# Gathers ahead of scatters, and new places for the re-layout of a mixture-of-experts block's tokens

## The chip, the cores and the metric

One core of a Trainium2 chip runs the program. The metric is the device time of one execution in microseconds (us). Five engines run instruction streams of their own, each in order: TensorE (PE, matmuls; its weight loads are listed as PEld), VectorE (DVE), ScalarE (ACT), GpSimd (POOL) and SyncE (SP, which here only issues DMA transfers). They meet at semaphores.

## The reference, cut to what matters

```python
x = A_x                                # 2048 tokens x 512
xn = layernorm(x)
return x + linear_attention(xn, A_wqkv, A_wo) + moe(xn, B_w_gate, B_w1, B_w2)

def moe(xf, w_gate, w1, w2):           # 8 experts, 512 -> 1792 -> 512, top 2 of 8
    logits = xf @ w_gate
    topk_idx = argsort(-logits)[:, :2]
    gates = softmax(top-2 logits)
    for e in range(8):
        w = (gates * (topk_idx == e)).sum(-1)
        out += w * (silu(xf @ w1[e]) @ w2[e])
```

## The kernel before, in words

The first 200 us are layer norm, linear attention and routing. Then come the experts, taken in the order of their token counts: **rank** r = 0 to 7, with room for 576, 552, 544, 528, 520, 512, 512 and 512 tokens (`CAP`). A rank has four blocks of 128 tokens, and ranks 0 to 4 a small fifth (`single(r)` is true where there is none).

The hidden width of 1792 is worked off in seven **pairs** j = 0 to 6 of 2 x 128 columns. From the third pair of the program on, one pair is `pair_fast` (line 1103): seven products of the first matmul by a Strassen-like scheme (PSUM tiles px, pz, px, pz, px, py, px, lines 1115), and between them pieces of the second matmul of the pair before (`mm2`, tiles y, lines 1044 and 1047). After product k it calls `jobs(k)`: the list of **slot** k (0 to 6), into which `plan` (line 1352) puts, with `on(k, f, ...)`, everything else of that stretch: splitting weights into a high and a low part, fetching weights, and the next rank's tokens. So a list written out by hand sets the order of the work on every queue; nothing is reordered later. The product py (line 1115, started after slot 4) writes into a PSUM tile that pz held, so it waits until DVE's line 1137 has read pz; that DVE instruction stands between slots 2 and 3.

The tokens of rank r + 1 are brought in during rank r, block by block (i = 0 to 4):
- `gather1` (line 899, the DMA at 904): an indirect DMA on POOL's queue fetches 128 rows from DRAM into a tile xg (pairs 0 and 1).
- `x_out` (line 954, DMAs at 959): SP stores the block to DRAM in four pieces of 64 KB, in another order (xs_d).
- `x_gate` (line 927, DVE at 933 and 934): two tiny DVE instructions take the block's gate values out of xg. `x_out` calls it at its end.
- `x_in` (line 964, DMA at 969): SP loads the block back, 256 KB, as xq; it can leave SP only when the block's stores have landed.
- `x_turn` (line 971, DVE at 978): two DVE 32x32 transpositions give the transposed operand xr.
- `x_hi`, `x_lo`, `x_sum` (pairs 4 to 6) make the operands of the products from xr.

The results go the other way. `put` (line 1013) scales a block of y by its gates into a tile yo, and POOL adds it to the output with an indirect scatter (line 1021). Rank r - 1's first two blocks (all four, for a rank of four blocks) are put at the start of pair 1 of rank r, the others (transposed first, `y_out`, line 1073) at the start of pairs 2 and 3. POOL works its queue in order: a gather behind a scatter waits until the scatter's data are there.

The tiles xg, xq and yo share one set of 11 buffers (`ta`, line 88). Weights go through three 512 KB staging buffers (`wst`); `fetch_w` (line 795) issues the next load on SP as soon as slot 4 (`w1_p_lo`) or slot 6 (`w2_lo`) has emptied one. All these DMAs of SP share one queue, in the order of issue.

Of the kernel before, what the change touches and what calls it, by code (L numbers as in the profile page):

```python
# [47 lines left out]
NP = NF // 2  # L48
NPLAIN = 2
BLK = 32  # L50
PRODUCTS = (("A11", "B11"), ("S1", "T1"), ("S2", "T2"), ("S4", "B22"),
            ("S3", "T3"), ("A12", "B21"), ("A22", "T4"))

# [6 lines left out]
def linear_attn_plus_moe(  # L60
# [46 lines left out]
    def psm(tag, name, n=512):  # L107
        bufs = {"acc": 4, "mm": 2, "tr": 2}[tag]
        t = ps.tile([P, 512], F32, tag=tag, name=name, bufs=bufs)
        return t[:, :n]  # L110
# [771 lines left out]
    def single(r):  # L882
        return CAP[r] == 4 * P

    def half(r):
        return CAP[r] // 2
# [8 lines left out]
    xg = {}  # L895
# [17 lines left out]
    def width(r, i):  # L913
        return P if i < 4 else CAP[r] - 4 * P

    def turned(r, q):
        if (r, "B11") not in XR:
            n = half(r)
            np_ = -(-CAP[r] // BLK) * BLK
            for q_ in range(2):  # L920
                t = raw(um(f"xr{r}_{q_}"))[:, :2 * np_].rearrange("p (k c) -> p k c", k=2)
                XR[r, q_] = t
                for c in range(2):
                    XR[r, f"B{q_ + 1}{c + 1}"] = t[:, :, c * n:(c + 1) * n]
        return XR[r, q]

    def x_gate(r, i):
        if i == 4 and single(r):
            return
        g, w = xg[r, i], width(r, i)  # L930
        b = r * RB + i
        g8 = wp.tile([P, E], F32, tag="g8", name=f"g8_{b}", bufs=2)
        V.tensor_tensor(g8[:w], g[:w, D:], ohr[:w, r, :], op=ALU.mult)
        V.tensor_reduce(gate[:w, b:b + 1], g8[:w], axis=AX.X, op=ALU.add)  # L934

    def x_block(r, i, tag="tr"):
        if i == 4 and single(r):
            return
        g, w = xg[r, i], width(r, i)
        p = psm(tag, f"xep{r}_{i}")  # L940
        for kc in range(KC):
            T.transpose(p[:, kc * P:(kc + 1) * P], g[:, kc * P:(kc + 1) * P], ident)
        p = p.rearrange("p (k c) -> p k c", k=KC)
        for q in range(2):
            A.activation(turned(r, q)[:, :, i * P:i * P + w], p[:, 2 * q:2 * q + 2, :w], AF.Copy)
        x_gate(r, i)
        xg.pop((r, i))

    xq = {}

    def groups(r, i):
        return -(-width(r, i) // BLK)

    def x_out(r, i):
        if i == 4 and single(r):
            return
        b = r * RB + i
        for c in range(groups(r, i)):
            Q.dma_start(xs_d[b * P:(b + 1) * P, c * P:(c + 1) * P].rearrange("(a j) f -> j a f", j=BLK),
                        xg[r, i][c * BLK:(c + 1) * BLK, :D].rearrange("p (a f) -> p a f", f=P))  # L960
        x_gate(r, i)
        xg.pop((r, i))

    def x_in(r, i):
        if i == 4 and single(r):
# [5 lines left out]
    def x_turn(r, i):  # L971
        if i == 4 and single(r):
            return
        ng = groups(r, i)
        src = xq.pop((r, i))[:, :ng * P].rearrange("p (c i k) -> p c k i", i=BLK, k=KC)
        for q in range(2):
            dst = turned(r, q)[:, :, i * P:i * P + ng * BLK].rearrange("p k (c j) -> p c k j", j=BLK)
            V.transpose(dst, src[:, :, 2 * q:2 * q + 2, :])  # L978
# [94 lines left out]
    def y_out(r, k, tag="mm"):  # L1073
        if single(r):
            return
        i, o, w = by_column(r)[k]
        p = psm(tag, f"yp{r}_{k}")
        for d in range(KC):
            T.transpose(p[:w, d * P:(d + 1) * P], yt[r, d // 2][:, d % 2, o:o + w], ident)  # L1079
        put(r, i, p, w, A)  # L1080
# [22 lines left out]
    def pair_fast(r, j, fill, jobs, held):  # L1103
# [5 lines left out]
        def product(k, ps_, start):  # L1109
            wn, xn_ = PRODUCTS[k]  # L1110
            which, o = WPOS[wn]
            w, x = W1[r, j][which], XF[r, xn_]
            for kc in range(2):
                for i, (a, b) in enumerate(PASSES):
                    T.matmul(ps_, w[a][:, o + kc, :], x[b][:, kc, :],  # L1115
                             start=(start and kc == 0 and i == 0), stop=(kc == 1 and i == 2),
                             skip_group_check=True)
# [92 lines left out]
    def q_transp(t):  # L1210
        p = psm("tr", f"pqp{t}")
        for kc in range(KC):
            T.transpose(p[:, kc * P:(kc + 1) * P], pz[t][:, kc * P:(kc + 1) * P], ident)  # L1213
        pqT[t] = sm(f"pqT{t}").rearrange("p (h c) -> p h c", h=2)
        split(pqT[t][:, 0], pqT[t][:, 1], p)
# [74 lines left out]
    for t in range(OLAG + 1, NT - 2):  # L1290
# [14 lines left out]
        if t == 12:  # L1305
            x_block(0, 0)
        if t == 13:
            x_block(0, 1)
            gather1(0, 4)
# [17 lines left out]
        if t == 13:  # L1327
            x_block(0, 2)


    t = NT - 2
# [20 lines left out]
    def plan(g):  # L1352

        r, j = pairs[g]
        at = [[] for _ in range(7)]
        front = []

        def on(k, f, *args):
            at[k].append(lambda: f(*args))

        if g + 1 < len(pairs) and g + 1 >= NPLAIN:
            nx = pairs[g + 1]
            on(0, w1_s_hi, *nx, 0)
            on(1, w1_s_hi, *nx, 1)
            on(1, w1_s_lo, *nx, 0)
            on(2, w1_s_lo, *nx, 1)
            on(2, w1_p_hi, *nx, 0)
            on(3, w1_p_hi, *nx, 1)
            on(3, w1_p_lo, *nx, 0)
            on(4, w1_p_lo, *nx, 1)  # L1370
        if g > 0:
            on(3, w2_hi, r, j, 0)
            on(4, w2_hi, r, j, 1)
            on(5, w2_lo, r, j, 0)
            on(6, w2_lo, r, j, 1)
        if g + 2 < len(pairs) and g + 2 >= NPLAIN:
            nx = pairs[g + 2]
            on(5, w1_sums, *nx, 0)
            on(6, w1_sums, *nx, 1)
        if g == 0:  # L1380
            for k, name in enumerate(("T1", "T3", "T2", "T4")):
                on(k, x_sum, 0, name)
        if g in (0, 1):
            for k, name in enumerate((("T1", "T2"), ("T3", "T4"))[g]):
                on(4 + k if g == 0 else 2 * k, x_hi, 0, name)
                on(5 + k if g == 0 else 2 * k + 1, x_lo, 0, name)
        if r + 1 < E:
            for i in {0: (0, 1), 1: (2, 3, 4)}.get(j, ()):
                on(1 + i, gather1, r + 1, i)
            for i in {1: (0, 1), 2: (2, 3, 4)}.get(j, ()):  # L1390
                on(0, x_out, r + 1, i)
                on(3, x_in, r + 1, i)
            for k, i in {2: ((1, 0), (2, 1)), 3: ((1, 2), (2, 3)), 4: ((0, 4),)}.get(j, ()):
                on(k, x_turn, r + 1, i)
            steps = {4: ((1, x_hi, "B11"), (4, x_hi, "B22"), (5, x_lo, "B11"), (6, x_sum, "T1")),
                     5: ((0, x_lo, "B22"), (0, x_sum, "T3"), (1, x_hi, "B21"), (4, x_hi, "T1"),
                         (5, x_lo, "B21"), (5, x_sum, "T2"), (6, x_lo, "T1")),
                     6: ((0, x_sum, "T4"), (1, x_hi, "T2"), (3, x_hi, "T3"), (4, x_hi, "T4"),
                         (5, x_lo, "T2"), (6, x_lo, "T3"))}
            for k, f, name in steps.get(j, ()):  # L1400
                on(k, f, r + 1, name)
        if r > 0 and j == 0:
            on(0, x_lo, r, "T4")
        if r > 0 and not single(r - 1):
            for k in {2: (0, 1), 3: (2,)}.get(j, ()):
                front.insert(k % 2, lambda k=k: y_out(r - 1, k))
        if j == 3 and r in (E // 2, E - 1):
            on(0, G.drain)
        if r == E - 1:
            if j == 2:  # L1410
                on(0, m_in)
            if 2 <= j < 5:
                for k in (0, 1):
                    if NO + 2 * (j - 2) + k < NT:
                        on(1 + k, pz_in, NO + 2 * (j - 2) + k)
            if j >= 4:
                for k in (0, 1):
                    if NO + 2 * (j - 4) + k < NT:
                        front.append(lambda k=k: q_transp(NO + 2 * (j - 4) + k))
        return at, front  # L1420
# [3 lines left out]
    held = None  # L1424
    for g, (r, j) in enumerate(pairs):
        at, front = plan(g)
        first = len(rest)
        todo = rest + (pieces(*pairs[g - 1]) if g else [])
# [110 lines left out]
```

## Time and profile before

| | |
|---|---|
| Median of 3 runs (lowest, highest) | 853.36 us (852.06, 854.20) |
| Profiled execution: its time, its span | 853.94 us, 852.30 us |
| PE busy | 837.9 us (98%) |
| DVE, ACT, POOL busy | 80%, 63%, 21% |
| Mean granted TensorE clock | 0.996 |
| DMA | 124.18 MB, mean 146 GB/s |

The span runs from the first to the last instruction; the execution's own time is 1.6 us longer. A row of a timeline gives the start and the length of an instruction (of several in a row, where it says xN), its engine and line, what it writes and reads, and in brackets how long the engine had been idle before it and what ended that. SPq is SP's sequencer issuing a DMA. Matmuls overlap: the length of one is more than the distance to the next.

### The profile page before, as it was taken

The numbers are of one execution on the slowest core, as the hardware profiler recorded it, in microseconds if no ns is written. First come the engines' busy times: TensorE is split into PE (matmuls) and PEld (weight loads), VectorE is DVE, ScalarE is ACT, GpSimd is POOL, SyncE is SP. The second block draws the span as 40 slices with busy tenths as digits, with TensorE's granted clock in tenths as the row PEclk, the third lists the DMA queues.
The fourth block names the chain that finished last, engine by engine and source line by source line (L and its number), as shares of the span: only waits on it lengthen the run. The fifth ranks groups of instructions, "written<-read, shape, count | busy, mean of one in ns | idle before, by whom it ended". The sixth has DMA issues, their size and how long they took to land.

```text
span 852.3 us, 15186 instructions
## 1 busy us (share of the span) xinstructions
PE 837.9 (98%) x5454; PEld 765.9 (90%) x5454; DVE 684.8 (80%) x1495; ACT 537.9 (63%) x1127; POOL 177.0 (21%) x200
## 2 busy tenths in 40 slices
PE   8999999999999999999999999999999979999997
PEld 7899878888899999999999999999989969999986
DVE  7888888988878887878787888778888867987741
ACT  5565464358566666776677677667767746776740
POOL 2432214464200240023004100310320040021011
PEclk9999999999999999999999999999999998999999
DMA  5541035463832584368338723943773383339306
GB/s 181 168 164 58 25 136 190 128 207 126 235 125 75 137 236 126 98 161 233 100 99 212 207 77 115 233 149 100 172 224 100 99 229 118 100 106 289 112 11 164
DMA packets 92640, 124.18 MB, mean 146 GB/s; under 512 B 10002, under 2 KB 55442, under 8 KB 92530
## 3 DMA queue, kind: packets, MB, share of 16 engines
q1 hardware_dynamic: 83858, 103.17, 39.9%
q0 software_dynamic: 7840, 18.57, 10.0%
q10 hardware_dynamic: 864, 1.44, 0.5%
q8 instruction: 44, 0.72, 0.3%
q14 instruction: 34, 0.28, 0.1%
HBM read 93.56 MB, written 30.91 MB: 146 GB/s over the span
## 4 chain that ended last, share of the span: by engine, by line
PE 87%; DVE 5%; DMA 3%; ACT 1%; POOL 1%; issue 1%; SPq 0%; POOLq 0%; DVEq 0%
PE y L1044 24%; PE px L1115 18%; PE y L1047 12%; PE pz L1115 9%; PE k L312 5%; PE py L1115 5%; PE op L1224 5%; PE qp L1173 4%; PE gacc L357 4%; DMA xg<-xn_d,gidx 2%; PE yp L1079 1%; PE pqp L1213 1%; PE xtp L274 1%; POOL out_dram L1021 1%; DMA xs_d<-xg 1%
## 5 line engine op out<-in xcount | busy, mean ns | idle before, releaser
L1021 POOL DMA_INDIRECT out_dram<-yo,sidx x37 | 61.1, 1652 | 504.6 <-DVE gate L934 273.1
L116 DVE TENSOR_TENSOR h<-hs,h 128x512 fp32r<-128x512 f32 (+5 forms) x112 | 78.8, 703 | 2.5 <-ACT h L113 1.7
L113 ACT ACTIVATE h<-hs 128x512 fp32r<-128x512 f32 (+5 forms) x112 | 72.5, 647 | 2.9
L1138 ACT ACTIVATE hs<-hs 128x256 f32<-128x256 f32 (+5 forms) x54 | 23.1, 427 | 64.3 <-DVE hs L1137 64.3
L1123 ACT ACTIVATE hs<-px 128x256 f32<-128x256 f32 (+5 forms) x54 | 21.1, 391 | 58.1 <-PE px L1115 58.1
L357 PE MATMUL gacc<-pkhl,xnhl 128*128 128x512 f32 x192 | 47.8, 398 | 0.0
L1142 DVE TENSOR_TENSOR hs<-px,hs 128x256 f32<-128x256 f32 (+5 forms) x54 | 23.4, 433 | 30.0 <-PE px L1115 29.0
L904 POOL DMA_INDIRECT xg<-xn_d,gidx x37 | 40.7, 1100 | 18.7 <-issue 7.5
L1137 DVE TENSOR_TENSOR hs<-pz,hs 128x256 f32<-128x256 f32 (+5 forms) x54 | 22.7, 421 | 25.8 <-PE pz L1115 25.8
L1148 DVE TENSOR_TENSOR hs<-py,hs 128x256 f32<-128x256 f32 (+5 forms) x54 | 23.4, 434 | 22.4 <-PE py L1115 22.3
L357 PEld LDWEIGHTS gacc<-pkhl,xnhl 128*128 128x128 f32 x192 | 34.9, 188 | 6.9 <-DVE pkhl L116 0.2
L978 DVE STREAM_TRANSPOSE xr<-xq 128x256 f32<-128x256 f32 (+2 forms) x64 | 34.3, 574 | 1.9 <-DMA xq<-xs_d 1.9
L1044 PE MATMUL y<-w_0h,h 128*128 128x512 f32 x88 | 33.8, 403 | 0.0
L1044 PE MATMUL y<-w_1h,h 128*128 128x512 f32 x88 | 33.6, 409 | 0.0
L1143 ACT ACTIVATE hs<-hs 128x256 f32<-128x256 f32 (+5 forms) x54 | 22.8, 423 | 15.7 <-DVE hs L1142 14.6
L1044 PE MATMUL y<-w_2h,h 128*128 128x512 f32 x88 | 32.5, 395 | 0.0
L1044 PE MATMUL y<-w_3h,h 128*128 128x512 f32 x88 | 32.5, 395 | 0.0
L1133 ACT ACTIVATE hs<-px 128x256 f32<-128x256 f32 (+5 forms) x54 | 21.2, 393 | 17.6 <-PE px L1115 16.7
L1044 PE MATMUL y<-w_4h,h 128*128 128x512 f32 x88 | 31.9, 394 | 0.0
L1044 PE MATMUL y<-w_6h,h 128*128 128x512 f32 x88 | 31.7, 394 | 0.0
L1044 PE MATMUL y<-w_5h,h 128*128 128x512 f32 x88 | 31.6, 393 | 0.0
L1182 ACT ACTIVATE e_q<-qp 128x512 f32<-128x512 f32 x16 | 9.6, 600 | 33.0 <-PE qp L1173 18.3
(517 smaller groups left out, 3106.5 us busy)
## 6 DMA issues: line engine op xcount, KB each, us to landing
wst<-in_B_w_dram SPq DMA_DIRECT2D x112, 512.0 KB
xs_d<-xg SPq DMA_DIRECT2D x117, 64.0 KB
xq<-xs_d SPq DMA_DIRECT2D x28, 256.0 KB
x<-in_A_x_dram SPq DMA_DIRECT2D x27, 256.0 KB
xn_d<-xn SPq DMA_DIRECT2D x16, 256.0 KB
out_dram<-x SPq DMA_DIRECT2D x11, 256.0 KB
out_dram<-zt SPq DMA_DIRECT2D x5, 256.0 KB
out_dram<-in_A_x_dram SPq DMA_DIRECT2D x1, 1280.0 KB
```

What stands on the lines that cost most here:

```text
L113: A.activation(hi, src, AF.Copy)
L116: V.tensor_tensor(lo, src, raw(hi), op=ALU.subtract)
L312: T.matmul(o, xT(t, a, kc), w[b][:, kc, :], start=(j == 0), stop=(j == 11))
L357: T.matmul(gacc[d], xnhl[:, a, d * P:(d + 1) * P], pkhl[:, b, :], start=(t == 0 and i == 0), stop=(t == NT - 1 and i == 2))
L904: G.indirect_dma_start(out=t, out_offset=None, in_=xn_d, in_offset=IOA(ap=gidx[:, b:b + 1], axis=0))
L978: V.transpose(dst, src[:, :, 2 * q:2 * q + 2, :])
L1021: st = G.indirect_dma_start(out=out, out_offset=IOA(ap=sidx[:w, b:b + 1], axis=0), in_=yo[:w], in_offset=None, compute_op=ALU.add).ins
L1044: T.matmul(ya[r, d], h[a][:, d * P:(d + 1) * P], w[b][:, n % 2, :], start=(first and i == 0), stop=(last and i == 2))
L1047: T.matmul(ya[r, d], w[a][:, n % 2, (d - nt) * P:(d - nt + 1) * P], h[b][:, nt * P:], start=(first and i == 0), stop=(last and i == 2))
L1115: T.matmul(ps_, w[a][:, o + kc, :], x[b][:, kc, :], start=(start and kc == 0 and i == 0), stop=(kc == 1 and i == 2), skip_group_check=True)
L1173: T.matmul(qp, xT(t, a, kc), wq_v[kc // 2][b][:, kc % 2, :], start=(kc == 0 and i == 0), stop=(kc == KC - 1 and i == 2))
L1224: T.matmul(op, pqT[t][:, a, kc * P:(kc + 1) * P], M_v[kc // 2][b][:, kc % 2, :], start=(kc == 0 and i == 0), stop=(kc == KC - 1 and i == 2))
```

## The change

The places of the five steps come from a table, `MOVES`, one for rank 0 and one for all later ranks: per pair a list of (slot, step, block), where g is `gather1`, o `x_out`, f `x_gate`, i `x_in`, t `x_turn`. For ranks after 0 all gathers move into pair 0 (slots 0 to 2). The stores of blocks 0 and 1 move from pair 1, slot 0, to pair 0, slot 5; those of blocks 2 to 4 from pair 2 to pair 1, slot 0. The loads move from slot 3 of pairs 1 and 2 to slots 1 and 4 of pair 1. Gates become steps of their own. Transpositions were at pair 2 (two), pair 3 (two) and pair 4 (the small one); they are now at pair 1 slot 5, pair 2 slot 2, pair 3 slot 1, and pair 4 slots 0 and 2. In rank 0 the gathers and stores stay where they were, the loads move one slot back, the gates of blocks 2 to 4 move behind line 1137 (pair 2, slot 3), and only one transposition is left in pair 2.

```diff
--- before.py
+++ after.py
@@ -48,6 +48,19 @@
 NP = NF // 2
 NPLAIN = 2
 BLK = 32
+MOVES = ({0: ((1, "g", 0), (2, "g", 1)),
+          1: ((0, "o", 0), (0, "o", 1), (1, "f", 0), (1, "f", 1), (3, "g", 2), (4, "i", 0),
+              (4, "i", 1), (4, "g", 3), (5, "g", 4)),
+          2: ((0, "o", 2), (0, "o", 3), (0, "o", 4), (2, "t", 0), (3, "f", 2), (3, "f", 3), (3, "f", 4),
+              (4, "i", 2), (4, "i", 3), (4, "i", 4)),
+          3: ((1, "t", 1), (2, "t", 2)),
+          4: ((0, "t", 3), (2, "t", 4))},
+         {0: ((0, "g", 0), (1, "g", 1), (1, "g", 2), (2, "g", 3), (2, "g", 4), (5, "o", 0), (5, "o", 1)),
+          1: ((0, "o", 2), (0, "o", 3), (0, "o", 4), (1, "i", 0), (1, "i", 1), (2, "f", 0), (2, "f", 1),
+              (4, "i", 2), (4, "i", 3), (4, "i", 4), (5, "t", 0)),
+          2: ((0, "f", 2), (0, "f", 3), (1, "f", 4), (2, "t", 1)),
+          3: ((1, "t", 2),),
+          4: ((0, "t", 3), (2, "t", 4))})
 PRODUCTS = (("A11", "B11"), ("S1", "T1"), ("S2", "T2"), ("S4", "B22"),
             ("S3", "T3"), ("A12", "B21"), ("A22", "T4"))
 
@@ -927,7 +940,7 @@
     def x_gate(r, i):
         if i == 4 and single(r):
             return
-        g, w = xg[r, i], width(r, i)
+        g, w = xg.pop((r, i)), width(r, i)
         b = r * RB + i
         g8 = wp.tile([P, E], F32, tag="g8", name=f"g8_{b}", bufs=2)
         V.tensor_tensor(g8[:w], g[:w, D:], ohr[:w, r, :], op=ALU.mult)
@@ -944,7 +957,6 @@
         for q in range(2):
             A.activation(turned(r, q)[:, :, i * P:i * P + w], p[:, 2 * q:2 * q + 2, :w], AF.Copy)
         x_gate(r, i)
-        xg.pop((r, i))
 
     xq = {}
 
@@ -958,8 +970,6 @@
         for c in range(groups(r, i)):
             Q.dma_start(xs_d[b * P:(b + 1) * P, c * P:(c + 1) * P].rearrange("(a j) f -> j a f", j=BLK),
                         xg[r, i][c * BLK:(c + 1) * BLK, :D].rearrange("p (a f) -> p a f", f=P))
-        x_gate(r, i)
-        xg.pop((r, i))
 
     def x_in(r, i):
         if i == 4 and single(r):
@@ -1385,13 +1395,9 @@
                 on(4 + k if g == 0 else 2 * k, x_hi, 0, name)
                 on(5 + k if g == 0 else 2 * k + 1, x_lo, 0, name)
         if r + 1 < E:
-            for i in {0: (0, 1), 1: (2, 3, 4)}.get(j, ()):
-                on(1 + i, gather1, r + 1, i)
-            for i in {1: (0, 1), 2: (2, 3, 4)}.get(j, ()):
-                on(0, x_out, r + 1, i)
-                on(3, x_in, r + 1, i)
-            for k, i in {2: ((1, 0), (2, 1)), 3: ((1, 2), (2, 3)), 4: ((0, 4),)}.get(j, ()):
-                on(k, x_turn, r + 1, i)
+            moves = MOVES[r > 0].get(j, ())
+            for k, f, i in moves:
+                on(k, (gather1, x_out, x_gate, x_in, x_turn)["gofit".index(f)], r + 1, i)
             steps = {4: ((1, x_hi, "B11"), (4, x_hi, "B22"), (5, x_lo, "B11"), (6, x_sum, "T1")),
                      5: ((0, x_lo, "B22"), (0, x_sum, "T3"), (1, x_hi, "B21"), (4, x_hi, "T1"),
                          (5, x_lo, "B21"), (5, x_sum, "T2"), (6, x_lo, "T1")),
```

## Rows read from the trace of the kernel before

**Rows 1.** The page of the profile: its totals (busy us, share of the span, instructions) and TensorE's granted clock, in tenths, in 40 equal slices of the span.

```profile
PE 837.9 (98%) x5454; PEld 765.9 (90%) x5454; DVE 684.8 (80%) x1495; ACT 537.9 (63%) x1127; POOL 177.0 (21%) x200
...
PEclk9999999999999999999999999999999998999999
```

**Rows 2.** Who TensorE waited for (us in total, times, longest us), the largest row.

```profile
PE py L1115 <- DVE hs L1137: 6.0, 2, 4.7
```

**Rows 3.** TensorE's timeline in pair 2 of rank 0 and in pair 2 of rank 6 (start, length, engine, line, what it writes and reads, idle before and releaser).

```profile
228.03 0.54 PE L1115 MATMUL py<-xB,wa_2h 128*128 128x288 f32 x2 [1.35 <-DVE hs L1137]
...
702.73 0.79 PE L1115 MATMUL py<-xB,wa_2h 128*128 128x256 f32 x2 [4.65 <-DVE hs L1137]
```

**Rows 4.** The chain that ended last, in order of time (start us, length us, what), in rank 6.

```profile
668.60 2.07 PE y L1044 x9
679.13 2.08 PE y L1044 x9
...
690.85 7.27 DMA xg<-xn_d,gidx
...
718.09 2.07 PE y L1044 x9
```

**Rows 5.** Busy time in stretches (stretch: its length, then busy us and instructions of PE, PEld, DVE, ACT and POOL, granted clock, DMA share, GB/s): pair 2 of rank 0, then rank 6.

```profile
223.00:228.00 5.00, 3.67 (x23) 3.15 (x21) 3.27 (x7) 0.78 (x2) 0.00 (x0) 1.00 0.88 270
...
680.00:690.00 10.00, 10.00 (x66) 9.06 (x65) 8.49 (x21) 7.66 (x17) 7.77 (x8) 1.00 0.77 174
690.00:700.00 10.00, 8.08 (x50) 6.93 (x48) 4.14 (x12) 3.34 (x8) 1.95 (x3) 1.00 0.98 293
...
703.00:709.00 6.00, 6.00 (x22) 5.26 (x23) 5.23 (x12) 3.84 (x9) 0.00 (x0) 0.57 0.51 161
...
720.00:730.00 10.00, 10.00 (x65) 9.10 (x64) 6.89 (x15) 7.64 (x17) 0.00 (x0) 1.00 0.37 106
```

**Rows 6.** DVE's timeline from the end of pair 1 to line 1137 of pair 2, rank 6.

```profile
689.24 0.42 DVE L845 TENSOR_TENSOR wr<-wst 128x256 f32<-128x256 f32 x1
...
690.03 0.68 DVE L116 TENSOR_TENSOR h<-hs,h 128x512 fp32r<-128x512 f32 x1
...
691.57 0.41 DVE L849 TENSOR_TENSOR wr<-wst,wr 128x256 f32<-128x256 f32 x1
696.00 0.17 DVE L933 TENSOR_TENSOR g<-xg,ohr 128x8 f32<-128x8 f32 x1 [4.01 <-DMA xg<-xn_d,gidx]
...
698.14 0.17 DVE L933 TENSOR_TENSOR g<-xg,ohr 128x8 f32<-128x8 f32 x1 [1.78 <-DMA xg<-xn_d,gidx]
...
698.42 0.68 DVE L116 TENSOR_TENSOR h<-hs,h 128x512 fp32r<-128x512 f32 x1
...
702.29 0.38 DVE L1137 TENSOR_TENSOR hs<-pz,hs 128x256 f32<-128x256 f32 x1
```

**Rows 7.** POOL's timeline: the first gather of two in rank 4, the last scatter of pair 3 in rank 5 and the gather behind it, and rank 6 its first scatter and its last gather.

```profile
560.87 1.27 POOL L904 DMA_INDIRECT xg<-xn_d,gidx  x1 [7.05 <-DVE hs L1148]
...
628.15 1.47 POOL L1021 DMA_INDIRECT out_dram<-yo,sidx  x1 [7.86 <-ACT yo L1017]
629.93 1.04 POOL L904 DMA_INDIRECT xg<-xn_d,gidx  x1 [0.30 <-DMA xq<-xs_d]
...
681.12 1.83 POOL L1021 DMA_INDIRECT out_dram<-yo,sidx  x1 [48.79 <-DVE yo L1019]
...
690.85 1.31 POOL L904 DMA_INDIRECT xg<-xn_d,gidx  x1 [0.30 <-issue]
```

**Rows 8.** Rank 0, pairs 1 and 2: two DMA steps of the chain (from the end of issue to landing), and DVE's transpositions.

```profile
217.61 5.00 DMA xs_d<-xg
...
222.75 3.71 DMA xq<-xs_d
...
223.42 1.19 DVE L978 STREAM_TRANSPOSE xr<-xq 128x256 f32<-128x256 f32 x2 [0.56 <-DMA xq<-xs_d]
...
226.49 1.14 DVE L978 STREAM_TRANSPOSE xr<-xq 128x256 f32<-128x256 f32 x2 [1.31 <-DMA xq<-xs_d]
```

**Rows 9.** DMA time from issue to landing, least, median and most: first the gathers (line 904), then the scatters (line 1021).

```profile
DMA to landing us min/median/max: 3.5/5.3/7.3
...
DMA to landing us min/median/max: 4.7/6.2/9.0
```

**Rows 10.** SP's timeline of DMA issues, rank 6, pairs 0 and 1 (line 811 and 808 weight loads, 959 stores).

```profile
677.14 0.38 SPq L811 DMA_DIRECT2D wst<-in_B_w_dram  x1
681.56 0.55 SPq L808 DMA_DIRECT2D wst<-in_B_w_dram  x1
682.15 4.76 SPq L959 DMA_DIRECT2D xs_d<-xg  x8
...
691.23 0.39 SPq L811 DMA_DIRECT2D wst<-in_B_w_dram  x1
```

**Rows 11.** The same steps in rank 5: SP's issues, DVE's line 846 in pair 1, and the first py of pair 2 on TensorE.

```profile
601.98 0.38 SPq L811 DMA_DIRECT2D wst<-in_B_w_dram  x1
...
606.21 5.22 SPq L959 DMA_DIRECT2D xs_d<-xg  x8
...
614.58 0.43 DVE L846 TENSOR_TENSOR wr<-wr,wst 128x256 f32<-128x256 f32 x1
...
623.71 0.40 PE L1115 MATMUL py<-xB,wa_2h 128*128 128x256 f32 x2
```

## The prediction, made before the changed kernel was run

> **What bounds the kernel now.** First the page's totals and its row of clock slices [rows 1]: TensorE (PE) is busy 98% of the span, and the clock is full in every slice but one. So a rearrangement of other queues can give back only PE's few gaps and the slow stretch behind one of them. Second, who PE waited for [rows 2]: of any size there is only the product called py, waiting for VectorE's (DVE's) line 1137, twice, 6.0 us. Third, PE's timeline at these two places [rows 3]: 1.35 us at 228 and 4.65 us at 703. The reader is to see that these are pair 2 of rank 0 and pair 2 of rank 6, and that pair 2 of ranks 1 to 5 has no such wait. Fourth, the chain [rows 4]: the triples "y x9" that open the pairs start at 668.60 and 679.13, a pair of 10.53 us. From 679.13 to 718.09 there are three pairs in 38.96 us, 7.37 more than three times 10.53. The wait is 4.65 of that; the rest, 2.7, is the clock. Over 703 to 709 the granted clock is 0.57 [rows 5], the lower level (1.2 GHz) for most of it, after PE had been idle 4.65 us; 43% of 6 us is 2.6 us. After the 1.35 us wait of rank 0 the clock stayed 1.00 [rows 5].
>
> What releases the 4.65 us is read backwards [rows 6]. DVE ends its line 849 at 691.98, then waits 4.01 and 1.78 us for two gathered blocks (the gate's line 933), ends the gates at 698.42 and comes to line 1137 at 702.29. Both gathers stand behind four scatters that start at 681.12; the second was issued at 690.85 [rows 7] and took 7.27 us to land [rows 4]. At 629.93 POOL had issued the first two gathers of the same rank at once after a scatter, 50 us before it was needed: what keeps a gather late is only that it stands behind the results of the rank before. In rank 0 there are no scatters; there DVE waits 1.31 us for xq (the block read back from DRAM), at 226.49, ahead of line 1137 [rows 8].
>
> **The change, part by part.** No instruction is added or removed; gathers, stores, loads, gates and transpositions only change places.
>
> *Gathers ahead of the scatters, ranks 1 to 6.* All four or five of the next rank are now queued in pair 0, before the first scatter of pair 1. POOL then issues them after the last scatter of pair 3 of the rank before, where the first two already go [rows 7]. Three more at about 1.3 us apiece, in a stretch in which POOL is idle 49 us: nothing on the path. They take their buffers from the 11 shared ones earlier; a gather that has to wait for one (bounds: nothing, or the 49 us that POOL has) holds up only scatters that are due 50 us later. I take nothing. Landing (3.5 to 7.3 us, [rows 9]) is then covered tens of us ahead, so the waits of 4.01 and 1.78 go, and the PE loss with its slow clock: **-7.4 us**, all in rank 6. In ranks 1 to 5 DVE's waits at the same gates had no PE wait behind them, so there the removal is worth nothing.
>
> *Gates moved* to slots 0 to 2 (rank 0: slot 3, behind line 1137): 0.28 us each (698.14 to 698.42, [rows 6]), as many as before, DVE not waiting: nothing.
>
> *Stores and loads moved up, one transposition into pair 1.* Here a new wait can arise: the first transposition now stands at slot 5 of pair 1, and DVE is in order. I work out when its data land in rank 6 [rows 10]. SP ends a weight load at 677.52; 8 stores took 4.76 us, 0.595 each, so the first eight are issued by 682.3, the next weight load (due 681.56) by 682.9, the other eight by 687.65. That weight load becomes 0.8 us later; it was asked for 7.7 us before line 845 reads such a load (689.24, [rows 6]) and DVE did not wait, so I take nothing (bounds: 0 and 0.8 us). The load at slot 4, at 691.23 now, is no longer behind a wait for stores and goes some 2 us earlier. So the first xq is issued at 687.7; no row shows how long it takes in that place. Nearest rows: 3.71 us for xq in rank 0 [rows 8]; from below 3.5, the fastest gather; from above 9.0, the slowest scatter [rows 9]. I take 3.7, since that is the same transfer in a stretch as full (DMA share 0.88 against 0.77 to 0.98, [rows 5]). It lands at 691.4.
>
> Without a wait, DVE would come to the transposition at 690.03, spend 1.05 us on it, 1.95 on what ran from 690.03 to 691.98, 0.56 on two gates, and on the steps from 698.42 to 702.29 (3.87) less one transposition 2.82 [rows 6]: line 1137 at 696.41, done at 696.8. PE had nothing left to do from 698.08 on (702.73 less 4.65, [rows 3]). So 1.3 us are free, the data may come at 691.3, and 691.4 costs PE 0.1 us. Rank 5, by the same steps [rows 11]: 602.36, 16 stores at 5.22/8, a weight load of 0.6: xq issued at 613.4, landed at 617.1; DVE reaches it at 615.0; then 1.05, 1.95, 0.56 and 2.82 give line 1137 at 623.5, done at 623.9, wanted at 623.71: 0.2 us. Ranks 1 to 4 run the same steps and have a fifth block's small stores more; I take 0.1 each. Together **+0.7 us**; with 3.5 us to land 0, with 9.0 some 5 us more in each of six ranks.
>
> The Trainium skill (DMA: Bandwidth & Descriptors, section "Anatomy of one DMA — SWDGE (gpsimd) path") fits a transfer as about 2.0 us and its bytes at 436 GB/s. That would be an estimated 2.6 us for the 256 KB of xq; the trace has 3.71, so the measurement decides here. By 2.6 the 0.7 us would be 0.
>
> *One transposition per pair.* Pair 2 loses one (1.05 us) ahead of line 1137, pair 3 loses one, pairs 1 and 4 gain one each. Line 1137 is what PE waits for; in pair 4 nothing new is waited for, and DVE idles 3.1 of its 10 us there [rows 5]. Nothing by itself; its gain is in the 2.82 above.
>
> *Rank 0.* The two transpositions ahead of line 1137 become one, the gates go behind it. The second xq (landing 226.46) is no longer waited for; the first landed by 223.42. The weight load that now goes ahead of xq is 512 KB at 270 GB/s [rows 5], 1.9 us, so xq may land at 225.3, the transposition end at 226.4, line 1137 at 226.8 against PE's 226.68. **-1.35 + 0.15 us.**
>
> Sum: -7.4 + 0.7 - 1.35 + 0.15 = -7.9 us. The profiled execution took 853.94 us (span 852.30, 1.6 around it), which gives 846.0; the median of the runs is 0.58 lower, 853.36: **845.5 us**.
>
> **Rivals.**
> 1. *No new wait at all* (xq lands in 3.5 us or the stores issue faster): -8.7, 844.6 us. For: the first eight stores now go where DMA is emptier. It lies inside the forecast's own range.
> 2. *The stall stays.* Two steps can keep it: a gather of rank 7 still waits, for a buffer, until the scatters come; or the gates find something else late. Then only rank 0's 1.2 us come back: 852.2. Against: two of those gathers went at 629.93 without such a wait. For: at 560.87 one waited 7.05 us for a release by DVE [rows 7].
> 3. *Slower: xq waits behind the stores in the rings.* Place: the transposition at slot 5 of pair 1, in ranks 1 to 6. Before, the load left SP only when its stores had landed; now eight stores and a weight load, 1.02 MB, go ahead of it. If none of that had moved when it is issued, it would take 3.5 us at 293 GB/s [rows 5] before xq's 3.7; the wait behind line 1137 grows to about 3.6 us in each of six ranks, 21.6 - 8.7 = +13 us, 866 (880 if each also costs the clock 2.7 us). It decides against the change once xq lands 1.5 us later than I take, in all six (8.7/6). Against: issue is spread over 10 us and stores landed 5.00 us after the last in the fullest stretch [rows 8], so most have drained by then.
> The Trainium skill (DMA: Bandwidth & Descriptors, section "Queues, rings and completion order") states that each DMA engine consumes one queue's descriptors in ring order; no row shows that order itself. By that rule rival 3 is the only open side of this change.
>
> **How the numbers follow.** A difference under 0.3% (2.6 us) can hardly be told here from none. Forecast with rival 1 (844 to 848.5): 0.72. Between it and 850.8, by xq landing about 1 us late: 0.05. Within 0.3%: rival 2, 0.07, and rival 3 half grown, 0.06. Rival 3 grown: 0.10. Faster 0.77, same 0.13, slower 0.10. The range goes from 844.0 (rival 1 less the runs' spread) to 851.0, which holds about 0.78 to 0.8.
>
> **What would show it.** PE's wait at py near 703 gone and the clock 1.00 there; five (four) gathers in a row right after the last scatter of pair 3, none after the scatters of pair 1; no DVE wait at line 933; at line 978 short waits for xq, once a rank, under 1.5 us. I am wrong if line 978 waits over 3 us with py waiting behind it, if a clock dip stands elsewhere, or if weight loads (wst) are waited for.

## The result, and the profile after

The changed kernel takes 858.09 us (median of 12 runs, 855.75 to 862.99), the kernel before 852.22 us beside it (12 runs, 848.26 to 856.38): ratio 1.0071, interval 1.0051 to 1.0090. It is **0.7% slower**, outside the predicted range, with the wrong sign. One execution of one kernel below (903.92 us, mean granted clock 0.85) is left out of its figures. In the profiled execution (856.67 us, span 855.0) lines stand 13 further down than before up to `x_gate`, 12 at the stores of `x_out` and 10 behind them: py is line 1125, the DVE line that it waits for 1147, the transposition 988, the split into high and low parts 126 and 129.

The page's totals and clock slices after, to be read against [rows 1]:

```profile
PE 837.6 (98%) x5454; PEld 764.5 (89%) x5454; DVE 684.3 (80%) x1495; ACT 538.7 (63%) x1127; POOL 177.9 (21%) x200
...
PEclk9999999999999999999999999999999999999999
```

TensorE does the same work; no slice shows the old dip. Who TensorE waited for (total, times, longest), against [rows 2]:

```profile
PE py L1125 <- DVE hs L1147: 3.7, 3, 3.2
PE y L1054 <- DVE h L129: 2.1, 1, 2.1
PE y L1057 <- DVE h L129: 1.9, 3, 1.1
```

The wait at py is shorter, but `y <- h` is new: pieces of the second matmul wait for DVE's split of h. DVE's own waits name the cause, a transposition that waits for xq seven times, once a rank:

```profile
DVE xr L988 <- DMA xq<-xs_d: 18.5, 7, 5.5
```

Before, DVE waited there 1.9 us in all (the row of the page: instructions, busy us and mean ns, then idle us before them):

```profile
L978 DVE STREAM_TRANSPOSE xr<-xq 128x256 f32<-128x256 f32 (+2 forms) x64 | 34.3, 574 | 1.9 <-DMA xq<-xs_d 1.9
```

Where the time went is read from the start of py in pair 3 of each rank (matmul timelines; "change" is after less before, cumulative; the other columns are other kernels' profiles less before's, which come below):

| rank | before, us | after, us | change | after again | rank 0 back | loads earlier | gathers only | transposition later | both repairs | gathers and rank 0 | before again |
|---|---|---|---|---|---|---|---|---|---|---|---|
| 0 | 240.00 | 242.78 | +2.78 | +4.18 | +0.69 | -0.26 | -0.18 | +0.75 | -0.64 | -1.15 | -0.63 |
| 1 | 322.93 | 326.39 | +3.46 | +4.18 | +0.68 | +0.74 | -0.08 | +0.75 | -0.64 | -1.15 | -0.63 |
| 2 | 403.49 | 407.66 | +4.17 | +5.12 | +0.68 | +1.39 | -0.09 | +0.75 | -0.64 | -1.15 | -0.64 |
| 3 | 482.30 | 487.82 | +5.52 | +6.08 | +1.49 | +2.39 | -0.09 | +0.74 | -0.65 | -1.15 | -0.59 |
| 4 | 559.28 | 564.81 | +5.53 | +7.29 | +3.31 | +2.43 | -0.08 | +0.75 | -0.64 | -1.15 | -0.57 |
| 5 | 634.72 | 640.81 | +6.09 | +7.52 | +3.63 | +3.74 | -0.09 | +0.74 | -0.64 | -1.15 | -0.57 |
| 6 | 715.81 | 717.47 | +1.66 | +2.77 | -0.67 | +1.58 | -7.43 | -5.76 | -3.88 | -8.51 | -3.98 |

So rank 0 lost 2.8 us, ranks 1 to 5 lost 3.3 (6.09 - 2.78), rank 6 gained 4.4. The last 1.1 us of the span's 2.7 comes behind the last py of rank 7, where the finished output is read back: its first load (xo) released DVE 5.7 us after its issue (840.93 to 846.59), before 4.5 us (839.32 to 843.83). In the six profiles with the first transposition in pair 1 and the scatters in place this load took 5.5 to 5.8 us, in the seven others 3.1 to 4.8; no experiment was made on why. The parts inside the ranks show in three places.

**The gathers** did what was predicted. POOL's timeline at the end of rank 5, against [rows 7]:

```profile
634.25 1.85 POOL L1031 DMA_INDIRECT out_dram<-yo,sidx  x1 [8.13 <-ACT yo L1027]
636.40 1.51 POOL L917 DMA_INDIRECT xg<-xn_d,gidx  x1 [0.30 <-issue]
638.22 1.29 POOL L917 DMA_INDIRECT xg<-xn_d,gidx  x1 [0.30 <-DVE xr L988]
639.81 1.01 POOL L917 DMA_INDIRECT xg<-xn_d,gidx  x1 [0.30 <-issue]
641.13 0.94 POOL L917 DMA_INDIRECT xg<-xn_d,gidx  x1 [0.30 <-DVE wa_4l L129]
```

All four gathers go in a row behind the last scatter of pair 3, and DVE waits at no gate any more.

**Rank 0.** SP's issues, then DVE, then TensorE around pair 2, against [rows 3, 8]:

```profile
218.17 0.41 SPq L824 DMA_DIRECT2D wst<-in_B_w_dram  x1
218.76 2.55 SPq L979 DMA_DIRECT2D xq<-xs_d  x2
```

```profile
227.94 1.14 DVE L988 STREAM_TRANSPOSE xr<-xq 128x256 f32<-128x256 f32 x2 [5.47 <-DMA xq<-xs_d]
229.00 0.42 DVE L1147 TENSOR_TENSOR hs<-pz,hs 128x288 f32<-128x288 f32 x1
```

```profile
229.47 0.85 PE L1125 MATMUL py<-xB,wa_2h 128*128 128x288 f32 x2 [3.16 <-DVE hs L1147]
```

The weight load (line 824) leaves at 218.17, ahead of the two xq loads at 218.76. The first xq releases DVE at 227.94: 9.2 us from the issue. Before, the same reading gave 3.9 (219.50 to 223.42, [rows 8]):

```profile
219.50 3.59 SPq L969 DMA_DIRECT2D xq<-xs_d  x2
```

The 3.71 us of [rows 8], on which the prediction built, are those of the second xq, and they run from the start of its issue (222.75), not from the end. Line 1147, in order behind the transposition, ends at 229.42, and TensorE has been idle 3.16 us. Two stretches after (busy us and instructions of PE, PEld, DVE, ACT and POOL, granted clock, DMA share, GB/s), against [rows 5]:

```profile
228.00:233.00 5.00, 3.53 (x16) 3.53 (x17) 4.86 (x16) 3.03 (x7) 1.92 (x2) 0.66 0.67 177
700.00:710.00 10.00, 7.88 (x48) 6.80 (x49) 9.70 (x24) 4.58 (x11) 0.00 (x0) 1.00 0.54 166
```

Behind that wait the granted clock is 0.66 over 228 to 233, most of it at the lower of its two levels (1.2 GHz). Rank 6, in 700 to 710, keeps 1.00.

**Rank 6.** SP's issues, DVE and TensorE, against [rows 6, 10]:

```profile
688.46 5.32 SPq L971 DMA_DIRECT2D xs_d<-xg  x8
693.90 0.86 SPq L979 DMA_DIRECT2D xq<-xs_d  x2
```

```profile
695.78 0.42 DVE L859 TENSOR_TENSOR wr<-wr,wst 128x256 f32<-128x256 f32 x1
700.07 1.14 DVE L988 STREAM_TRANSPOSE xr<-xq 128x256 f32<-128x256 f32 x2 [3.87 <-DMA xq<-xs_d]
701.13 0.65 DVE L129 TENSOR_TENSOR h<-hs,h 128x512 fp32r<-128x512 f32 x1
...
706.40 0.38 DVE L1147 TENSOR_TENSOR hs<-pz,hs 128x256 f32<-128x256 f32 x1
```

```profile
701.84 0.50 PE L1054 MATMUL y<-w_1h,h 128*128 128x512 f32 x1 [2.12 <-DVE h L129]
...
706.84 0.50 PE L1125 MATMUL py<-xB,wa_2h 128*128 128x256 f32 x2 [0.28 <-DVE hs L1147]
```

SP issues the first xq at 693.90; less the 6.09 us by which the rank starts later that is 687.8, and 687.7 was predicted. DVE has nothing else from 696.20 on and waits 3.87 us. The first thing behind the transposition is not line 1147 but the split of h (701.13; before it is the row at 690.03 in [rows 6]), and TensorE waits for that split, 2.12 us; py later waits only 0.28. In ranks 1 to 3 it is the same, shorter; rank 3, on DVE and on TensorE:

```profile
468.44 1.16 DVE L988 STREAM_TRANSPOSE xr<-xq 128x256 f32<-128x256 f32 x2 [2.37 <-DMA xq<-xs_d]
```

```profile
470.25 0.39 PE L1057 MATMUL y<-h,w_1h 128*128 128x272 f32 x1 [1.06 <-DVE h L129]
```

DVE idles 2.37 us for xq, TensorE 1.06 us for h. In ranks 1, 2, 4 and 5 DVE idled 1.86, 1.85, 0.73 and 2.37 us; TensorE 0.40, 0.44, nothing, and 0.27 (at py). These waits add up to 2.2 us, the starts of py in the table move by 3.3: matmuls overlap, so an idle time is shorter than the delay behind it.

### The profile page after: what moved, and what is told of

It is laid out like the page before. It is cut to its first block, busy times and chain, and to the rows that moved or that the text cites. A ratio compares the mean times of both kernels' runs of the same rounds, so it can differ in the third digit from the quotient of the medians.

```text
span 855.0 us, 15184 instructions
## 1 busy us (share of the span) xinstructions
PE 837.6 (98%) x5454; PEld 764.5 (89%) x5454; DVE 684.3 (80%) x1495; ACT 538.7 (63%) x1127; POOL 177.9 (21%) x200
```

## The experiments

The theory after this result: the early gathers are worth what was forecast, and two other parts of the change lose it again, the loads of rank 0 that stand behind a weight load, and the transposition at slot 5 of pair 1, which stands in DVE's queue ahead of the low part of h. Against it: that the early gathers themselves do harm (they take buffers and DMA time), or that the stores and loads, wherever DVE stands, crowd the DMA queue. In the kernels of the experiments line numbers are again others: py is line 1114, line 1137 of before 1136, the transposition 977, the splits 115 and 118, y 1043 and 1046.

**Rank 0 back.** Only the table of rank 0 as before:

```diff
 MOVES[rank 0]
-1: ... (1, "f", 0), (1, "f", 1), (4, "i", 0), (4, "i", 1)
-2: ... (2, "t", 0), (3, "f", 2 to 4), (4, "i", 2 to 4)
-3: (1, "t", 1), (2, "t", 2)    4: (0, "t", 3), (2, "t", 4)
+1: ... (0, "f", 0), (0, "f", 1), (3, "i", 0), (3, "i", 1)
+2: ... (0, "f", 2 to 4), (3, "i", 2 to 4), (1, "t", 0), (2, "t", 1)
+3: (1, "t", 2), (2, "t", 3)    4: (0, "t", 4)
```

> The changed kernel with rank 0's table put back to the places of before (loads of xq one slot earlier and so ahead of the weight load, stores' gates with them, two transpositions in pair 2); ranks 1 to 6 as changed. In the profile of the changed kernel rank 0 is 2.8 us longer than before, because its first xq takes 9.2 us to land. Theory T (rank 0's own new order does it: the weight load goes ahead of xq, and the load is later): rank 0 is as before again, 2.8 us off the changed kernel, about 855. Rival G (the gathers of rank 2, which POOL now runs ahead with, all five of them, into rank 0's fullest stretch): xq still lands late, time as the changed kernel's 858 or longer, since two transpositions now wait.

Measured: 856.06 us (11 runs), ratio 1.0054 (1.0036 to 1.0072), 2.0 us under the changed kernel between medians, where theory T had 2.8 and rival G none. xq released DVE 4.6 us after its issue, so it was not late as the rival had it. In the table above, rank 0 loses 0.7 instead of 2.8, and the loss of ranks 1 to 5 stays at 2.9 (3.63 - 0.69): that part is not rank 0's.

**Rank 0 only.** The kernel before, with the new table of rank 0 alone.

> The kernel before with only rank 0's new table; ranks 1 to 6 as before. T: rank 0 pays its 2.8 us, all else as before: about 855 (852.2 + 2.8). G: only two gathers of rank 2 run ahead, as before, so xq lands as before and the time is 851 to 852, rank 0's 1.35 us wait being gone or smaller. In either case the stall of pair 2 in rank 6 stays (4 to 7 us in the profile).

Measured: 853.86 us (12 runs), ratio 1.0028 (1.0008 to 1.0047). xq was issued at 219.72 and released DVE at 226.13, 6.4 us, without a loss in rank 0 (0.28 us gained in the profile, where 2.8 lost were expected); the old stall of rank 6 stays, as it must. By the ratio this part alone costs 2.4 us (0.28%), between medians 1.4 (852.43 before), which the one profile doesn't show; where it goes in other executions stays open. So does why xq landed sooner here than in the full change (9.2): there POOL has issued a gather of rank 2 more by then, but one profile doesn't settle it.

**Gathers only.** The kernel before, with all gathers of the later ranks in pair 0:

```diff
 MOVES[later ranks], from the places of before
-0: (1, "g", 0), (2, "g", 1)    1: (3, "g", 2), (4, "g", 3), (5, "g", 4), ...
+0: (0, "g", 0), (1, "g", 1), (1, "g", 2), (2, "g", 3), (2, "g", 4)    1: ...
```

> The kernel before with one edit: in ranks 1 to 6 all gathers of the next rank stand in pair 0, ahead of the scatters; stores, loads, gates, transpositions and rank 0 as before. If the early gathers are the gain that was forecast and the new places of the other steps are the loss: the stall of rank 6 goes (7.4 us in the profile, perhaps less in the mean of the unprofiled runs, which spread from 848 to 856), no wait at line 978's transpositions in ranks 1 to 6: 845 to 847 by T; by G rank 0 pays some 3 us for the gathers of rank 2: 848 to 850.

Measured: 848.91 us (12 runs), ratio 0.9956 (0.9940 to 0.9972), a gain of 3.5 us between medians; the profiled execution took 846.78. TensorE's wait at py in its profile, against [rows 2]:

```profile
PE py L1114 <- DVE hs L1136: 0.9, 2, 0.7
```

Rank 6 gains 7.34 us in this profile (-7.43 less -0.09), the predicted term, and no other rank loses. The median lies in the range that was given to the rival (848 to 850), but the loss in rank 0 that was to explain it is not in this profile. That early gathers never cost rank 0 anything is not shown: with the same table of rank 0 and the same gathers it lost 0.69 us in the run with rank 0 back and 2.29 in the one that comes next, against 0 and -0.63 in the two profiles of the kernel before.

**Transposition where it was.** The kernel with rank 0 back, and the first transposition of later ranks again at pair 2, slot 1:

```diff
 MOVES[later ranks]
-1: ... (5, "t", 0)    2: (0, "f", 2), (0, "f", 3), (1, "f", 4), (2, "t", 1)
+1: ...                2: (1, "t", 0), (0, "f", 2), (0, "f", 3), (1, "f", 4), (2, "t", 1)
```

> As the first of these (rank 0 as before), and in ranks 1 to 6 the first transposition goes from pair 1, slot 5, to pair 2, slot 1, where it was; stores and loads stay early. If the transposition that waits for xq ahead of the split of h is what costs 0.4 to 2.4 us a rank (3.3 us over ranks 1 to 5, 2.4 in rank 6): 5 us under the first of these, 848 to 851. If the cost is the crowding of DMA by early stores, it stays within 2 us of it.

Measured: 848.81 us (11 runs), ratio 0.9949 (0.9931 to 0.9967), against 856.06 with the transposition at slot 5. Stores and loads stand in both where the change put them, and ranks 1 to 5 lose nothing now: it is the place in DVE's queue, not the crowding. In this profile rank 0 lost 2.29 us though its table is that of before (xq 218.35 to 225.20, 6.9 us): how long this load takes varies by itself.

**Transposition one slot later.** The whole change, with one number changed:

```diff
 MOVES[later ranks]
-1: ... (4, "i", 4), (5, "t", 0)
+1: ... (4, "i", 4), (6, "t", 0)
```

> The changed kernel with one edit: in ranks 1 to 6 the first transposition goes from slot 5 to slot 6 of pair 1, so behind the split of h (the h_lo that PE waited for at 308, 390, 470 and 702) and not ahead of it. It still waits for xq and still stands ahead of line 1137. If it is h_lo that PE waits for: the waits of y for h go in all ranks; ranks 1 to 3 are as before (2.7 us less), in ranks 5 and 6 a wait at py through line 1137 may stay (0.3 and 1 to 2 us): 858 less 3 to 4, 854 to 855. If lateness of DVE as a whole is what counts, as I had it: the waits move to py and the time stays at 857 to 858.

Measured: 849.65 us (12 runs), ratio 0.9974 (0.9962 to 0.9987): 8.4 us under the changed kernel between medians, more than twice what was expected. Slot 6 is called after `h_lo`, slot 5 before it. Rank 6 on DVE, then on TensorE:

```profile
690.77 0.68 DVE L118 TENSOR_TENSOR h<-hs,h 128x512 fp32r<-128x512 f32 x1
...
694.50 1.16 DVE L977 STREAM_TRANSPOSE xr<-xq 128x256 f32<-128x256 f32 x2 [1.77 <-DMA xq<-xs_d]
...
698.97 0.38 DVE L1136 TENSOR_TENSOR hs<-pz,hs 128x256 f32<-128x256 f32 x1
```

```profile
699.41 0.51 PE L1114 MATMUL py<-xB,wa_2h 128*128 128x256 f32 x2 [0.59 <-DVE hs L1136]
```

The split of h (690.77) goes ahead, DVE waits 1.77 us for xq behind it, and TensorE stops at no y, only 0.59 us at py. Ranks 1 to 5 lose nothing. Of the 7.4 us between the profiles' tables at rank 6 (1.66 to -5.76), 3.3 are ranks 1 to 5 and 2.1 rank 6; the other 2.0 are rank 0, where this kernel differs in nothing: its xq took 7.9 us instead of 9.2.

**Loads of rank 0 earlier.** The whole change, with the loads of rank 0 at slot 3, ahead of the weight load:

```diff
 MOVES[rank 0]
-1: ... (4, "i", 0), (4, "i", 1)    2: ... (4, "i", 2 to 4)
+1: ... (3, "i", 0), (3, "i", 1)    2: ... (3, "i", 2 to 4)
```

> The changed kernel with one edit: in rank 0 the loads of xq stand at slot 3 of their pairs, as before, so ahead of the weight load of slot 4; one transposition, the gates behind line 1137 and all of ranks 1 to 6 as changed. xq took 9.2 us to land in rank 0 of the changed kernel and 6.4 with rank 0's new table alone, both behind a weight load; 3.9 to 4.6 in three of four profiles with the loads ahead (6.9 in the fourth). If the weight load ahead is the cause: xq lands in 4 to 5 us, rank 0 loses its 2.8 us and, with one transposition, up to 1.3 more: about 855. If the five gathers of rank 2 in that stretch are: xq stays over 6 us and the time at 857 to 858.

Measured: 854.33 us (12 runs), ratio 1.0016 (0.9991 to 1.0040), 3.8 us under the changed kernel between medians. SP's issues:

```profile
218.72 3.09 SPq L968 DMA_DIRECT2D xq<-xs_d  x2
222.06 0.39 SPq L813 DMA_DIRECT2D wst<-in_B_w_dram  x1
```

xq now goes first, the weight load at 222.06, and DVE has xq 6.3 us after issue (225.05), not the 4 to 5 that were expected. In the table rank 0 gains 0.26 us instead of losing 2.8, but one pair later it is 0.57 behind: ScalarE waits for a weight load, which now stands behind the loads of xq on SP, and TensorE for the split of h behind that. ScalarE, then TensorE:

```profile
242.32 0.63 ACT L115 ACTIVATE w_3h<-wst 128x512 fp32r<-128x512 f32 x1 [2.99 <-DMA wst<-in_B_w_dram]
```

```profile
245.71 0.41 PE L1046 MATMUL y<-h,w_3h 128*128 128x320 f32 x1 [0.38 <-DVE h L118]
```

The waits for h in later ranks stay, up to 3.5 us in rank 6, so that this profile (856.80 us) ends rank 6 where the changed kernel's does (+1.58 against +1.66); the 3.8 us are a difference of medians. TensorE's waits for h:

```profile
PE y L1043 <- DVE h L118: 4.0, 2, 3.5
PE y L1046 <- DVE h L118: 2.5, 5, 0.8
```

**Both repairs.** The whole change with both of these edits, rank 0's loads at slot 3 and the transposition at slot 6.

> The changed kernel with two edits: in rank 0 the loads of xq at slot 3 (they alone brought 858 to 854), and in ranks 1 to 6 the first transposition at slot 6 of pair 1, behind the split of h (that alone brought 849.7). If these two places carry the whole loss of the change: the two gains add, 858.1 - 3.8 - 8.4 = 845.9, as good as the version with only the gathers moved and rank 0 mended (845.8). If something else in the early stores and loads costs time: 848 or more.

Measured: 847.91 us (12 runs), ratio 0.9946 (0.9929 to 0.9962). The two gains don't add up to 845.9: the interval is 846.4 to 849.2 us, so these two places carry most of the loss and not all of it. The profiled execution was the slowest of them, 851.18, and shows what is left in rank 6, on DVE and TensorE:

```profile
694.88 1.14 DVE L977 STREAM_TRANSPOSE xr<-xq 128x256 f32<-128x256 f32 x2 [3.54 <-DMA xq<-xs_d]
```

```profile
699.75 0.50 PE L1114 MATMUL py<-xB,wa_2h 128*128 128x256 f32 x2 [2.32 <-DVE hs L1136]
```

xq was issued at 687.55 and took 7.3 us. DVE waited 3.54 us and py 2.32, and the granted clock was 0.83 over 700 to 710. So even behind the split of h the transposition in pair 1 depends on a landing that varies.

**Without the scatters.** The changed kernel, where `put` returns ahead of the scatter in ranks 0 to 5, so that these results are never added; the rest runs.

```diff
 def put(r, i, ...):
     ...
+    if r < 6:
+        return
```

> The changed kernel without the indirect scatters of the results of ranks 0 to 5 (they are left out; those of ranks 6 and 7 stay). If the scatters that run beside the loads are what makes xq late (6.2 us in rank 6, where four run in a row, 3.6 to 4.9 us in ranks 1 to 5, where two do): xq lands in about 3.5 us in every rank from 2 on, and DVE's wait at the first transposition falls from 1.9 to 3.9 us to about 1. If it is the queue of stores and weights ahead of the load: the waits stay within 0.5 us. Rank 0, which has no scatters beside it, stays as it is in both.

Measured, one run: 850.24 us. Rank 6, SP and DVE:

```profile
690.35 0.94 SPq L979 DMA_DIRECT2D xq<-xs_d  x2
```

```profile
693.36 0.42 DVE L859 TENSOR_TENSOR wr<-wr,wst 128x256 f32<-128x256 f32 x1
693.70 1.15 DVE L988 STREAM_TRANSPOSE xr<-xq 128x256 f32<-128x256 f32 x2
```

Issued at 690.35, xq was there when DVE reached it at 693.70, with no wait: at most 3.35 us, where the changed kernel has 6.2 beside four scatters issued at 687.22 to 693.11. DMA in that time, then in the changed kernel while its xq was on its way (columns as above):

```profile
690.35:693.70 3.35, 3.35 (x23) 3.00 (x22) 2.46 (x7) 2.76 (x7) 0.00 (x0) 1.00 0.77 202
```

```profile
694.00:700.00 6.00, 5.72 (x35) 4.78 (x34) 1.78 (x4) 3.52 (x8) 0.72 (x2) 1.00 1.10 252
```

The DMA share is 0.77 without the scatters and 1.10 with them. In rank 6 xq is there some 4 us sooner without them: 1.1 us because it is issued sooner (690.35 less the 3.67 by which the rank starts later is 686.7, against 687.8), the rest because it takes less time. Whether the scatters do that by their engine time or by their order in the queues the run doesn't tell, and it is one run. In ranks 1 to 5, beside two scatters, it shows no such thing: where DVE waited xq took 3.4 to 5.1 us without them and 3.6 to 4.9 with them, so the expected 3.5 in every rank did not come. No wait for h is left among TensorE's, and the gain of rank 6 is 7.36 us. Rank 0 is as slow as in the changed kernel (+2.84), with no scatter in either: there it is another cause.

**Gathers, and rank 0 with its loads ahead.** What the runs point to: the gathers of later ranks in pair 0, everything else of later ranks as before; for rank 0 the new table with loads at slot 3.

> The version that the runs point to: in ranks 1 to 6 only the gathers ahead of the scatters (the edit of the run that had only that, 848.9), and in rank 0 one transposition in pair 2, the gates behind line 1137 and the loads of xq at slot 3. Rank 0 then waits for nothing: up to 1.3 us under that run, 847.5 to 849.

Measured: 845.80 us (5 runs, 844.73 to 846.31), ratio 0.9921 (0.9905 to 0.9937). It beats both kernels, and the forecast's best (847.5) by 1.7 us. Its profile explains 1.1 of the 3.1 us against the gathers alone (rank 0, -1.15 less -0.09). Where the rest comes from is not shown; with the old table of rank 0 and early gathers, rank 0 cost between -0.09 and 2.29 us in three profiles. Of the waits on DVE in the experts one remains:

```profile
PE y L1046 <- DVE h L118: 0.2, 1, 0.2
```

**Both kernels profiled again.** They tell how far one profile is to be trusted.

> The kernel before once more, for a second profile of it: its unprofiled runs spread from 848.3 to 856.5, and the first profile, at 853.9, had 7.4 us in the stall of rank 6. If that spread is the stall itself (how late the two gathers land): rank 6 shows another length, between 3 and 9 us, and the rest of the ledger of pairs agrees within 0.5 us. If it lies elsewhere: rank 6 shows 7.4 us again.

> The changed kernel once more, for a second profile: unprofiled it takes 858.1 us in the median, its first profile 856.7. If the waits for xq are what varies: rank 0's 2.8 us and rank 6's wait of 2.4 us differ by a microsecond or more from the first profile, and the waits stand in the same places (line 988 behind xq in pair 2 of rank 0 and pair 1 of ranks 1 to 6).

Measured: before 849.95 us, after 857.58. The chain and TensorE of the kernel before in rank 6, against [rows 3, 4]:

```profile
689.95 5.08 DMA xg<-xn_d,gidx
```

```profile
699.67 0.79 PE L1115 MATMUL py<-xB,wa_2h 128*128 128x256 f32 x2 [2.16 <-DVE hs L1137]
```

The same gather took 5.08 us instead of 7.27, py waited 2.16 instead of 4.65, and the table's last column has rank 6 some 3.4 us shorter (-3.98 + 0.57). The other ranks agree within 0.06 us, rank 0 within 0.63. The changed kernel lost at the same places again: 4.18 in rank 0 (xq 9.9 us, py 3.8), 3.3 in ranks 1 to 5, and gained 4.75 in rank 6. Rank 0 differs by 1.4 us from the first profile, as expected, but TensorE's waits in rank 6 by only 0.3 (1.78 and 0.28 against 2.12 and 0.28). The first profiles of the two kernels are 2.7 us apart, the second ones 7.6, the medians of 12 runs 5.9: how long the old stall was in the profile that is compared makes most of that.

## Why the prediction was wrong, step by step

**Gathers ahead of the scatters, -7.4 us:** the mechanism is shown (gathers only: -7.34 in the profile, no loss elsewhere). Its size was read from an execution at the upper part of a spread: the stall cost 7.4 us there and 4.0 in the second profile, and between medians the step is worth 3.5 us. Of the gain in the changed kernel 4.4 and 4.75 us are left in rank 6, behind the new wait there. "The stall stays" did not come.

**Stores, loads and the transposition moved up, +0.7 us:** this step failed, in two places. First the deadline. I counted the time until line 1137 must run; but `h_lo` is called behind slot 5, so the split of h, which TensorE needs for y 4.7 us sooner (701.84 against 706.84 less 0.28), stood behind the transposition. That split is in the sum, in the 1.95 us "on what ran from 690.03 to 691.98", but as work without a deadline of its own. The forecast of DVE's own wait in rank 5 was good, 2.1 us (617.1 less 615.0) against 2.37, by luck in part: xq was issued 0.9 us sooner than forecast and took 4.9 us instead of 3.7. Who pays for it was wrong. In place of the 0.6 us that the sum has for ranks 1 to 5, they lost 3.3 us in both profiles, and one slot later that loss is gone. Second, the landing: 3.7 us taken, 6.2 measured in rank 6, and 5.8 to 7.4 in the other runs with the transposition in pair 1 and the scatters beside it; at most 3.35 without the scatters, in one run. That bound (up to 9.0) was in the text, the value taken from a stretch without scatters.

**Rank 0, -1.35 + 0.15 us:** failed too. I let the weight load cost xq its own 1.9 us. Loads issued behind it took 6.4 to 9.9 us in five profiles, those ahead of it 3.9 to 6.9 in eight. The loss is 2.8 and 4.2 us in the two profiles of the changed kernel, the clock's share included (2.84 without the scatters, 0.75 with the transposition one slot later, a gain of 0.28 with rank 0 alone). With the loads ahead and the rest of the new table it goes from a gain of 1.15 us to a loss of 0.57, where a weight load is waited for instead. The early gathers of rank 2, which I took as free, may have a part in it: behind the weight load xq took 6.4 us with two of them and 7.9 to 9.9 with all five, ahead of it 3.9 and 5.9 with two and 4.3 to 6.9 with five. With equal gathers the two orders don't overlap, and xq was issued at 218.4 to 219.8 in all; the part of the gathers rests on one profile. The Trainium skill (DMA: Bandwidth & Descriptors, section "Queues, rings and completion order") has each DMA engine consume one queue's descriptors in ring order. The two groups agree with that, though over all runs their ranges overlap and no run shows the order itself.

**Rival 3** (slower, xq late behind stores and weight load) had the right kind and sign at 0.10, half grown at 0.06. Its place was wrong: it is rank 0 that pays for the weight load, rank 6 for the scatters (by one run), and ranks 1 to 5 pay through h even with xq landing in 3.1 to 5.1 us (both profiles). The Trainium skill's fit (the same page, section "Anatomy of one DMA — SWDGE (gpsimd) path") would give an estimated 2.6 us for such a load, though the page gives it for transfers that GpSimd issues and xq is issued by SP. Two landings agree with it: the second xq of rank 0 released DVE 2.67 us (gathers only, 222.85 to 225.52) and 2.58 us (transposition where it was, 224.68 to 227.26) after its issue. No first xq of a rank whose landing could be read took less than 3.1.

**What the predicted signs showed:** the gathers in a row and no wait at the gate came true. "Line 978 waits over 3 us" was the sign of being wrong, and it came in ranks 0 and 6, with py behind it in rank 0. The clock dip "elsewhere" came too (0.66 behind that py), while the clock near 703 was 1.00 as forecast. That TensorE would wait for h was not on the list.

What stays open: why xq varies between 6.4 and 9.9 us in rank 0 behind the same weight load, the 2.4 us that rank 0's table costs alone, the 2.0 us by which the two repairs together fall short of their sum, and why the output is read back later at the end.

## What to carry to other kernels

When a step that may wait is moved up in an in-order queue, list every instruction behind it with its own deadline; the nearest consumer decides, not the one that bound before. A load's time to land belongs to its place, to what is ahead of it in its queue and what runs beside it, so take it from rows of that place or keep the whole range. And a stall made of a transfer's landing should be sized from more than one execution.

## What the runs showed of the hardware

- The same 256 KB load took 3.9 to 9.9 us in one place of the program (the first block in rank 0), 5.8 to 7.4 us beside four accumulating scatters (rank 6, six profiles), and at most 3.35 without them (one profile).
- A wait of TensorE of about 2 us did or did not lower the granted clock: 2.12 us (after, rank 6) and 2.19 (transposition one slot later, rank 0, over 228 to 233) left it at 1.00; 2.15 (transposition where it was, rank 0) was followed by 0.66 over 228 to 233, and 2.16 (before again) and 2.32 (both repairs) by 0.85 and 0.83 over 700 to 710. 1.35 us left it at 1.00 and 4.65 gave 0.57 [rows 3, 5].
